# Reordering the start of a two-layer attention and gMLP kernel: x, wq and wk loaded first, one weight scaled at a time, the other weights' loads tied to the loop's steps

## The chip, the cores and the metric

The kernel runs on one core of a Trainium2 chip. The metric is the device time of one execution in microseconds (us). The engines of the core work beside each other and wait for each other through semaphores: TensorE (PE, matrix products; PEld is its loading of weights), VectorE (DVE), ScalarE (ACT), GpSimd (POOL), and SyncE (SP), whose queue issues the DMA transfers of this kernel one after the other.

## The reference

The input x is 2048 × 640 in float32. Four residual steps follow, an attention A and a gated MLP B, each twice with the same weights:

```python
x = x + A(layernorm(x));  x = x + B(layernorm(x))
x = x + A(layernorm(x));  x = x + B(layernorm(x))

def A(x):                      # 32 heads of 20, 4 segments of 512 rows
    q, k, v = x @ wq, x @ wk, x @ wv          # each 640 x 640
    for s in range(4):
        a_dot = softmax(q_s k_s^T * 20**-0.5 + causal mask) @ v_s
        a_mem = phi(q_s) M / (phi(q_s) z + 1e-6)
        o_s   = g * a_mem + (1 - g) * a_dot   # g = sigmoid(beta), by head
        M, z  = M + phi(k_s)^T v_s, z + sum(phi(k_s))
    return o @ wo

def B(x):                      # w_in 640 x 1728, w_sp 2048 x 2048, w_out 864 x 640
    z = gelu(x @ w_in)
    return (z[:, :864] * (w_sp @ layernorm(z[:, 864:]) + b_sp)) @ w_out
```

## The kernel before

All large products are made of 16-bit halves: each float32 operand is scaled and split into a high and a low part (h and l at the end of a tile's name), and three products are summed. A weight is scaled by a power of two that comes from its largest absolute value. For one weight that is: loads of 128 × 640 rows into a staging tile, a maximum of each on DVE, `pow2_scales` (a transpose and a product on PE and seven small instructions on DVE, lines 52 to 65, ending in `iv`), and `split_scaled` for each of five row blocks (high part on ACT, line 72; low part on DVE, line 73).

`prologue` does this for wv, wq and wk at the start (loads line 135, maxima line 138), and makes some scalars from the scales (lines 150 to 165). Each layer is then one attention (`Attention.run`), one stretch for the output projection and w_in, and one for w_sp and w_out. The weights wo, w_in and w_out are split once and the halves are kept in DRAM; the second layer loads these (line 96).

In the attention, x comes in 16 tiles of 128 rows, four to a segment. `prep` loads a tile (line 608), takes its statistics (lines 202 to 205), normalizes it (line 616), splits it (lines 217, 218) and turns it by a DMA transpose (line 219). `value(t)` makes the values of a tile (vps, 30 matmuls, line 633). `unit(s, m)` makes q and k of segment s for 128 of the 640 columns (qps and kps, 15 matmuls each, line 690), which go as qhl and khl (line 707) to a stack in DRAM (`st`, lines 799, 800), and phi of k as phl (line 724). Each of the 64 head pairs (16 per segment) then fetches its rows from the stack (`qk<-st`, line 810), is multiplied for its row maxima (mp, line 828; mx on DVE, line 872), gets its `mr` (DVE, line 893, with the transfer `qk<-mr` to the pair's tile), and makes and uses its probabilities (P, PH, PL, pv). One mr stands for one pair, so these instructions mark progress.

The loop in `run` has three steps t to a pair, from a negative start to about 200. At each step, four generators add work that is due: `fills` (prep of later x tiles, loads of o), `background`, `dense` (values and units of the next segment) and `reads`. `background` is tied to steps only by the number it yields. At its start it runs `other_scales`: 32 loads of wo, w_in and w_out into two staging buffers (tile `wmst`, line 179), each with a maximum (`wap`, lines 181 and 185), and the scale chain at step 53. From step 55 on it loads and splits wo and the second half of w_in (tiles `wst`, lines 106, 72, 73) and stores the halves (line 111); in the second layer it loads them.

The order on PE is the program's own: `manual_schedule(engines=ENGINES)` holds only PE to it. For DVE, ACT, POOL and SP a list scheduler sets the order, by priority and by when it expects an operand. What is due at a later step of `background` can therefore stand far ahead of that step on SP and DVE.

## Time and profile before

| | us |
|---|---|
| three runs before, median (lowest to highest) | 2440.96 (2439.71 to 2448.43) |
| the profiled execution's own time | 2440.32 |
| its span in the trace | 2438.6 |
| PE busy | 2218.2 |
| DVE busy | 1434.3 |
| first value matmul | 36.33 |
| first matmul of unit (0,2) | 88.20 |
| mr of pair 1, first attention | 123.85 |
| mr of pair 1, second attention | 1313.42 |

The page gives busy time by engine, the chain of work that ended last, and the costliest groups of instructions. A group's row reads: line, engine, operation, output<-inputs, shapes, count | busy us, mean ns of one | idle time of the engine ahead of them and what ended it. A row of the table of windows reads: stretch, its length, busy us of PE, PEld, DVE, ACT and POOL with the number of instructions, PE's granted clock, busy share of the DMA engines, GB/s. A row of the timeline reads: start, duration, engine, line, operation; SPq is the issue of a transfer. A row of the chain reads: start, length, what it was.

### The profile page before, as it was taken

To read this page: it belongs to the slowest core of one execution; us is meant where nothing else is said; L and a number is where in the kernel's file an instruction comes from. 1 tells how busy PE (TensorE), PEld (TensorE's weight loads), DVE (VectorE), ACT (ScalarE), POOL (GpSimd) and SP (SyncE) were. 2 spreads that over 40 slices of the span, in tenths; PEclk is the share of its full clock that TensorE was granted. 3 is DMA by queue.
4 is the path that set the end of the run, shared out by engine and by line. 5 is a ranking of instruction groups with operands and counts; after the bars stand their busy time and mean duration, and the time that the engine had idled before them with its cause. 6 is when DMAs were issued, how large, how long until landed. Compare 5 with 4: busy or idle time off the path is not lost.

```text
span 2438.6 us, 50718 instructions
## 1 busy us (share of the span) xinstructions
PE 2218.2 (91%) x20682; PEld 1319.0 (54%) x20682; DVE 1434.3 (59%) x2766; ACT 1133.7 (46%) x1388; POOL 936.1 (38%) x728
## 2 busy tenths in 40 slices
PE   3698789999899989999997989999988997999998
PEld 2355455666555545555554556565654554555554
DVE  8668878777654555444326777877764452454441
ACT  3278777777632222212124988777762221121110
POOL 3168678888610100000002988887871010000000
PEclk9899999999999999999999999999998998999999
DMA  6824634344553488766445253443455345665762
GB/s 196 214 57 109 162 115 122 93 117 133 146 143 107 113 223 206 171 157 164 114 127 133 77 119 88 113 109 93 123 160 124 88 108 165 163 169 155 175 127 58
DMA packets 502505, 325.00 MB, mean 133 GB/s; under 512 B 408512, under 2 KB 443456, under 8 KB 497152
## 3 DMA queue, kind: packets, MB, share of 16 engines
q1 hardware_dynamic: 502272, 321.76, 51.4%
q8 instruction: 162, 2.65, 0.5%
q14 instruction: 71, 0.58, 0.1%
HBM read 148.25 MB, written 85.34 MB: 96 GB/s over the span
## 4 chain that ended last, share of the span: by engine, by line
PE 60%; DVE 11%; DMA 11%; ACT 7%; issue 5%; POOL 3%; SPq 3%; ACTq 0%; DVEq 0%; POOLq 0%
PE gp L380 16%; PE zp L295 14%; PE cyp L409 6%; PE pv L909 3%; PE yps L666 3%; PE kps L690 3%; DMA wr<-in_B_w_sp_dram 3%; PE vps L633 3%; PE mp L856 3%; PE qps L690 3%; ACT PH L882 2%; ACT P L865 2%; PE es L856 2%; POOL PL L883 2%; DVE mx L872 2%
## 5 line engine op out<-in xcount | busy, mean ns | idle before, releaser
L883 POOL TENSOR_TENSOR PL<-P,PH 128x1280 f16<-128x1280 f32 x248 | 649.8, 2621 | 155.2 <-ACT PH L882 145.6
L380 PE MATMUL gp<-zh,wt 128*128 128x432 f16 x2048 | 466.5, 348 | 24.0 <-DMA wt<-wn 24.0
L872 DVE TENSOR_REDUCE mx<-mp 128x2 f32<-128x1024 f32 (+3 forms) x512 | 409.4, 818 | 108.1 <-PE mp L828 106.2
L380 PEld LDWEIGHTS <-wt 128*128 128x128 f16 x3072 | 301.8, 98 | 286.5 <-DMA wt<-wn 25.7
L865 ACT ACTIVATE P<-es,sc 128x1024 f32<-128x1024 f32 (+1 forms) x384 | 370.3, 964 | 128.5 <-PE es L828 122.6
L882 ACT CAST PH<-P 128x1280 f16<-128x1280 f32 x256 | 320.5, 1253 | 19.0 <-PE pv L909 12.0
L295 PEld LDWEIGHTS <-th 128*128 128x128 f16 x1920 | 188.9, 99 | 177.8 <-issue 11.7
L380 PE MATMUL gp<-zl,wt 128*128 128x432 f16 x1024 | 272.8, 348 | 0.0
L395 POOL MEMSET un<- 128x64 f16 x32 | 4.8, 151 | 675.7 <-DMA ut<-un 588.9
L205 POOL TENSOR_TENSOR lnrs<-lnve,mhalf 128x1 f32<-128x1 f32 x96 | 58.6, 618 | 484.6 <-DVE lnve L204 459.6
L856 PEld LDWEIGHTS <-qk 60*128 60x128 f16 (+1 forms) x2048 | 93.0, 94 | 222.2 <-issue 155.1
L357 DVE TENSOR_REDUCE am<-wr 128x1 f32<-128x2048 f32 x32 | 73.2, 2286 | 214.7 <-DMA wr<-in_B_w_sp_dram 214.6
L383 ACT ACTIVATE u<-gp,bsp,un 128x864 f32<-128x864 f32 x32 | 34.2, 1068 | 355.5 <-PE gp L380 355.5
L409 PE MATMUL cyp<-wuh,ut 128*128 128x320 f16 (+1 forms) x896 | 166.8, 303 | 15.4 <-DMA ut<-un 15.4
L633 PE MATMUL vps<-wvh,xt 128*128 128x320 f16 x640 | 156.3, 310 | 22.5 <-DMA xt<-xnhl 13.8
L856 PE MATMUL es<-qk 64*128 64x512 f16 (+3 forms) x1024 | 135.2, 299 | 41.6 <-ACT P L865 26.9
L409 PEld LDWEIGHTS <-ut 128*128 128x128 f16 (+1 forms) x1344 | 132.6, 99 | 73.7 <-DMA ut<-un 17.4
L909 PE MATMUL pv<-vs,PL 128*128 128x41 f16 x2560 | 163.8, 181 | 7.3 <-POOL PL L883 4.5
L909 PE MATMUL pv<-vs,PH 128*128 128x41 f16 x2560 | 167.8, 182 | 1.2 <-DVE ab L925 1.2
L828 PEld LDWEIGHTS <-big 64*128 64x128 f16 x3072 | 141.7, 95 | 49.8 <-issue 3.1
L856 PE MATMUL mp<-qk 60*128 60x512 f16 (+3 forms) x1024 | 137.8, 306 | 31.1 <-DVE mx L872 28.6
L367 ACT ACTIVATE wn<-wr,ivw 128x1024 f16<-128x1024 f32 x64 | 71.9, 1144 | 194.6 <-DVE ivw L362 111.1
(182 smaller groups left out, 4138.5 us busy)
## 6 DMA issues: line engine op xcount, KB each, us to landing
wr<-in_B_w_sp_dram SPq DMA_DIRECT2D x32, 1024.0 KB
qk<-st SPq DMA_DIRECT2D x256, 120.0 KB
x<-x SPq DMA_DIRECT2D x56, 320.0 KB
z<-z SPq DMA_DIRECT2D x32, 432.0 KB
cz<-z SPq DMA_DIRECT2D x32, 432.0 KB
xt<-in_A_x_dram SPq DMA_DIRECT2D x32, 320.0 KB
st<-qhl SPq DMA_DIRECT2D x40, 256.0 KB
st<-khl SPq DMA_DIRECT2D x40, 256.0 KB
```

The costliest lines, as they stand in the source:

```text
L295: nc.tensor.matmul(zp[:, n, :FHH], a[:, k, :], b[:, k, c:c + FHH], start=(k == 0 and j == 0), stop=(k == KD - 1 and j == 2))
L380: nc.tensor.matmul(gp[:, n, :FHH], wt[:, k // 8, a, k % 8, :], b[:, k, n * FHH:(n + 1) * FHH], start=(k == 0 and j == 0), stop=(k == NT - ...
L409: nc.tensor.matmul(yp[:, n, :320], a[:kn[k], k, :], b[:kn[k], k, n * 320:(n + 1) * 320], start=(k == 0 and j == 0), stop=(k == KO - 1 and ...
L633: nc.tensor.matmul(ps, a[:, k, c], b[:, k, n * 320:(n + 1) * 320], start=(i == 0), stop=(i == 14))
L690: nc.tensor.matmul(ps, a[:, k, c], b[:, k, :], start=(i == 0), stop=(i == 14))
L828: nc.tensor.matmul(out, g.big[r, 64 - 64 * s:192 - 64 * s], mk, start=False, stop=s == 1, skip_group_check=True)
L856: nc.tensor.matmul(out[:, h, o:o + w], a[r, ac], b[r, bc], start=o == 0, stop=False, skip_group_check=True)
L865: nc.scalar.activation(P[:, :, 512 * c:512 * c + ew], es[:, :, :ew], AF.Exp, scale=g.esc)
L872: nc.vector.tensor_reduce(self.mx[m][:, :, i], mp[:, :, o:o + w], AX.X, ALU.max)
L882: nc.scalar.copy(PH, P[:, h])
L883: (nc.gpsimd if h == 0 or n < self.N - self.TAIL else nc.vector).tensor_tensor(PL, P[:, h], PH, ALU.subtract)
L909: nc.tensor.matmul(pv[:, i, h, :], x[:, c:c + 128], v[:, j, h0 + h, :], start=(j == 0 and x is PH), stop=(j == i and x is PL), skip_group_ ...
```

## The change

`prologue` becomes `attn_weights`, which only makes tiles, `attn_scalars`, and a method `head` that the first attention runs ahead of its loop, at high priority. `head` loads the first four x tiles, then wq and wk; the wv loads are held behind the last transpose of x. The four tiles get one power instruction together. The weights are then taken one at a time: maxima of q, scale of q, split of q, maxima of k behind the second split of q, and so on, with the four unit products of (0,0) and (0,1) placed between. The values of the four tiles come last.

`other_scales` starts at step −10 with three quarters of a step between loads. Each of its maxima is held behind the last mx or vs instruction of DVE added so far (`self.dve`), and whatever `fills` and `background` add is held behind the last fetch or mr transfer of SP (`self.sp`). That hold applies to both attentions. Memory for wo and the second half of w_in is opened after the head.

```diff
...
-def prologue(g, ctx, wv, wq, wk, wo, w_in, w_out):
+def attn_weights(g, ctx, wv, wq, wk, wo, w_in, w_out):
 
     nc, tc = g.nc, g.tc
-    wp = ctx.enter_context(tc.tile_pool(name="wqkv", bufs=1))
-    g.w = {}
+    wp = ctx.enter_context(tc.tile_pool(name="wqkv", bufs=1, reuse_waits="tile"))
+    g.raw = {"q": wq, "k": wk, "v": wv}
+    g.w = {nm: tuple(wp.tile([128, KD, D], F16, name=f"w{nm}{p}") for p in "hl") for nm in "vqk"}
...
-    nc.vector.memset(g.wap, 0.0)
     g.wam = wp.tile([128, 8], F32, name="wam")
-    with tc.tile_pool(name="wpro", bufs=1, side="right", reuse_waits="tile") as p, \
-            tc.tile_pool(name="wpp", bufs=1, space=PSUM, reuse_waits="tile") as pp:
-        am = p.tile([128, 4, KD], F32, name="wamk")
-        st = {}
-        for i, (nm, dram) in enumerate((("v", wv), ("q", wq), ("k", wk))):
-            st[nm] = p.tile([128, KD, D], F32, name="wst" + nm)
-            for k in range(KD):
-                nc.sync.dma_start(st[nm][:, k, :], dram[k * 128:(k + 1) * 128, :])
-        for i, nm in enumerate("vqk"):
-            for k in range(KD):
-                nc.vector.tensor_reduce(am[:, i, k:k + 1], st[nm][:, k], AX.X, ALU.max, apply_absolute_value=True)
-            nc.vector.tensor_reduce(g.wam[:, i:i + 1], am[:, i], AX.X, ALU.max)
-            pow2_scales(g, p, pp, "wsc", g.wam, i, 1)
-            h = wp.tile([128, KD, D], F16, name=f"w{nm}h")
-            l = wp.tile([128, KD, D], F16, name=f"w{nm}l")
-            for k in range(KD):
-                split_scaled(g, h[:, k], l[:, k], st[nm][:, k], i)
-            g.w[nm] = (h, l)
-
-    pq, pk = g.pw[:, 1:2], g.pw[:, 2:3]
...
+def attn_scalars(g):
+
+    nc = g.nc
+    pq, pk = g.pw[:, 1:2], g.pw[:, 2:3]
...
-def other_scales(g, stage, pool, psum, tag):
+def other_scales(g, a, pool, psum, tag):
 
     nc = g.nc
     last = None
...
         for k in range(w.nk):
             n = min(128, w.dram.shape[0] - 128 * k)
             for c in range(0, w.cols, width):
-                t = stage.tile([128, D], F32, tag="bg", name="wmst")[:n, :width]
+                t = a.bg.tile([128, D], F32, tag="bg", name="wmst")[:n, :width]
                 nc.sync.dma_start(t, w.dram[k * 128:k * 128 + n, w.c0 + c:w.c0 + c + width])
                 if last is not None:
-                    nc.vector.tensor_reduce(*last, AX.X, ALU.max, apply_absolute_value=True)
+                    with g.tc.issue_after(a.dve):
+                        nc.vector.tensor_reduce(*last, AX.X, ALU.max, apply_absolute_value=True)
                 last = g.wap[:n, i, j:j + 1], t
                 yield True
                 j += 1
...
+    def head(self):
+
+        g, nc, tc = self.g, self.nc, self.tc
+        abs_max = lambda out, a: nc.vector.tensor_reduce(out, a, AX.X, ALU.max, apply_absolute_value=True)
+        with ExitStack() as ctx:
+            p = ctx.enter_context(tc.tile_pool(name="wpro", bufs=1, side="right", reuse_waits="tile"))
+            ctx.enter_context(tc.high_priority(offset=HP))
+            xs = self.p3.tile([128, 4, D], F32, tag="P", name="xs")
+            hl = self.p3.tile([128, 4, 2, D], F16, tag="P", name="xhl")
+            for t in range(4):
+                nc.sync.dma_start(xs[:, t], self.x[t])
+            st = {nm: p.tile([128, KD, D], F32, name="wst" + nm) for nm in "qkv"}
+
+            def load(nm):
+                for k in range(KD):
+                    self.sp = nc.sync.dma_start(st[nm][:, k, :], g.raw[nm][k * 128:(k + 1) * 128, :]).ins
+
+            def largest(nm, behind):
+                a = p.tile([128, KD], F32, tag="wamk" + nm, name="wamk")
+                with tc.issue_after(behind):
+                    for k in range(KD):
+                        nc.vector.tensor_reduce(a[:, k:k + 1], st[nm][:, k], AX.X, ALU.max, apply_absolute_value=True)
+                i = WNAMES.index(nm)
+                return nc.vector.tensor_reduce(g.wam[:, i:i + 1], a, AX.X, ALU.max).ins
...
+            load("q")
+            load("k")
+            sx = p.tile([128, 4, 2, 6], F32, name="sx")
+            mv = p.tile([128, 4, 2], F32, name="mvx")
+            rs = p.tile([128, 4], F32, name="rsx")
+            for t in range(4):
+                for i in range(2):
+                    nc.vector.bn_stats(sx[:, t, i, :], xs[:, t, i * 320:(i + 1) * 320])
+                nc.vector.bn_aggr(mv[:, t], sx[:, t])
+            nc.vector.tensor_scalar(rs, mv[:, :, 1], EPS, XS ** -2, ALU.add, ALU.mult)
+            nc.gpsimd.tensor_tensor(rs, rs, g.mhalf.to_broadcast((128, 4)), ALU.pow)
+            for t in range(4):
+                i = nc.vector.tensor_scalar(xs[:, t], xs[:, t], mv[:, t, 0:1], rs[:, t:t + 1], ALU.subtract, ALU.mult)
+                nc.scalar.copy(hl[:, t, 0], xs[:, t])
+            for t in (2, 0, 3, 1):
+                (nc.gpsimd if t > 1 else nc.vector).tensor_tensor(hl[:, t, 1], xs[:, t], hl[:, t, 0], ALU.subtract)
+            for t in (0, 1, 2, 3):
+                o = self.xt[0][:, :, :, t * 128:(t + 1) * 128]
+                last = nc.sync.dma_start(o.rearrange("p i k c -> p (i k) c"), hl[:, t].rearrange("p i c -> p (i c)"), transpose=True).ins
+            with tc.issue_after(last):
+                load("v")
+            qp = self.pe.tile([128, 2, 512], F32, tag="es", name="qp")
+            kp = self.px.tile([128, 2, 512], F32, tag="mp", name="kp")
+            largest("q", i.ins)
+            scale("q")
+            i = split("q")
+            largest("k", i[1])
+            units("q", 0, qp)
+            scale("k")
+            units("q", 1, qp)
+            i = split("k")
+            attn_scalars(g)
+            largest("v", i[-1])
+            units("k", 0, kp)
+            scale("v")
+            units("k", 1, kp)
+            split("v")
+            for t in range(4):
+                for _ in self.value(t):
+                    pass
+                if t == 0:
+                    self.start()
 
     def prep(self, t):
...
                         yield 3 * 136
...
-                nc.vector.scalar_tensor_tensor(v[:, :, DH + 1:], ps, QS, v[:, :, 0:DH], ALU.mult, ALU.subtract)
+                self.dve = nc.vector.scalar_tensor_tensor(v[:, :, DH + 1:], ps, QS, v[:, :, 0:DH], ALU.mult, ALU.subtract).ins
...
-    def unit(self, s, m):
+    def unit(self, s, m, own=None):
 
         g, nc = self.g, self.nc
         xh, xl = self.xt[s % 2][:, 0], self.xt[s % 2][:, 1]
-        for nm in ("q", "k"):
+        for nm in ("q", "k") if own is None else own:
             wh, wl = g.w[nm]
-            ps = self.pd.tile([128, L], F32, tag="dn", name=f"{nm}ps")
+            ps = self.pd.tile([128, L], F32, tag="dn", name=f"{nm}ps") if own is None else own[nm]
...
-            self.nc.sync.dma_start(self.qk[n % self.NQK][64 * h:64 * h + 60], self.st[n // 16 % 2][c:c + 20].rearrange("p l i c -> (p l) i c"))
+            self.sp = self.nc.sync.dma_start(self.qk[n % self.NQK][64 * h:64 * h + 60], self.st[n // 16 % 2][c:c + 20].rearrange("p l i c -> (p l) i c")).ins
 
...
-                nc.vector.tensor_reduce(self.mx[m][:, :, i], mp[:, :, o:o + w], AX.X, ALU.max)
+                self.dve = nc.vector.tensor_reduce(self.mx[m][:, :, i], mp[:, :, o:o + w], AX.X, ALU.max).ins
...
-            nc.sync.dma_start(self.qk[n % self.NQK][60 + i:125 + i:64, 0].rearrange("h (t c) -> h t c", t=4), mr[:, i])
+            self.sp = nc.sync.dma_start(self.qk[n % self.NQK][60 + i:125 + i:64, 0].rearrange("h (t c) -> h t c", t=4), mr[:, i]).ins
...
         def background():
 
-            g = self.g
-            yield 6
+            g, nc = self.g, self.nc
+            yield -10
             if not g.wo.made:
-                for i, _ in enumerate(other_scales(g, self.bg, self.pl1, self.pm, "ms")):
-                    yield 6 + 1.2 * i if _ else 53
+                nc.vector.memset(g.wap, 0.0)
+                for i, _ in enumerate(other_scales(g, self, self.pl1, self.pm, "ms")):
+                    yield -10 + 0.75 * i if _ else 53
+                nc.sync.dma_start(g.bsp, self.b_sp.rearrange("(t p) -> p t", p=128))
             yield 54
             for j, (w, width, pace) in enumerate(((g.wo, D, 1.3), (g.wi[1], FHH, 3))):
                 w.tiles(g.top[j])
...
                     yield 55 + 14 * j + pace * i
 
         if self.stacked < 0:
-            for t in range(0, 4, 2):
-                for f in zip(self.prep(t), self.prep(t + 1)):
-                    f[0]()
-                    f[1]()
-                if t == 0:
-                    self.start()
-            for i in range(4, 8):
-                self.early(i)
+            self.head()
         else:
             self.start()
+        g = self.g
+        g.top = [self.top.enter_context(g.tc.tile_pool(name=n, bufs=1, side="right", reuse_waits="tile")) for n in ("topi", "topo")][::-1]
         streams = [[next(it), i, it] for i, it in enumerate((fills(), background(), dense(), reads()))]
 
         def until(t):
...
                 e = min(streams)
                 if e[0] >= t:
                     return
-                e[0] = next(e[2], None)
+                with self.tc.issue_after(self.sp) if e[1] < 2 and self.sp is not None else ExitStack():
+                    e[0] = next(e[2], None)
                 if e[0] is None:
                     streams.remove(e)
...
```

Three places show the order. The first is PE at the start; wtp and wbc are the two products of a scale chain. Before, the last two chains and the first value product:

```order
L58 MATMUL wbc<-wdg,ones_68 128x1
L52 MATMUL wtp<-ident,wam 1x128
L58 MATMUL wbc<-wdg,ones_68 128x1
L633 LDWEIGHTS xt_302
L633 MATMUL vps<-wvh,xt_302 128x320
```

After, the end of the first product of q (qp), the chain of k and the beginning of the second:

```order
L757 MATMUL qp<-xt_172,wqh 128x512
L757 LDWEIGHTS wql
L757 MATMUL qp<-xt_172,wql 128x512
L52 MATMUL wtp<-ident,wam 1x128
L58 MATMUL wbc<-wdg,ones_68 128x1
L757 LDWEIGHTS wqh
L757 MATMUL qp<-xt_172,wqh 128x512
```

Before, three scale chains are followed by 120 matmuls for values and then by those of units (0,0) and (0,1), 15 for each q and k. After, the chain of q is followed by 15 matmuls for q, the chain of k, 15 for q and 15 for k, the chain of v, the last 15 for k, and then the 120 for values. From unit (0,2) on both are the same.

The second place is the start of SP's queue, with the loads of weights, x and wmst. Before:

```order
L479 DMA gate<-in_A_beta_dram 128x32
L135 DMA wstv<-in_A_wv_dram 128x640 x5
L135 DMA wstq<-in_A_wq_dram 128x640 x5
L135 DMA wstk<-in_A_wk_dram 128x640 x5
L1108 DMA bsp<-in_B_b_sp_dram 128x16x1
L608 DMA xt<-in_A_x_dram 128x640 x2
L179 DMA wmst<-in_A_wo_dram 128x640 x5
```

After:

```order
L601 DMA xs<-in_A_x_dram 128x640 x4
L606 DMA wstq<-in_A_wq_dram 128x640 x5
L606 DMA wstk<-in_A_wk_dram 128x640 x5
L466 DMA gate<-in_A_beta_dram 128x32
L645 DMA_TRANSPOSE xt_172<-xhl 128x10x128 x4
L606 DMA wstv<-in_A_wv_dram 128x640 x5
```

x stands first, wv behind the transposes, and wmst comes later: two loads before the first pair's fetches and nine more before the first mr transfer, where there were 32.

The third place is DVE around the first mr instruction. Before, at the last maxima (line 185 is the last of them, line 187 begins the scale chain):

```order
L181 TENSOR_REDUCE wap<-wmst 128x1
L616 TENSOR_SCALAR xt<-xt,lnmv,lnrs 128x640
L185 TENSOR_REDUCE wap<-wmst 96x1
L187 TENSOR_REDUCE wam<-wap 128x4
L872 TENSOR_REDUCE mx<-mp 128x2 x2
L788 TENSOR_TENSOR mst_299<-mup,bmask 128x147
L707 SCALAR_TENSOR_TENSOR khl<-kps,khl 128x512
L712 TENSOR_SCALAR kps<-kps,sc 128x512
```

After, from the first mr on (line 960 is now mr, 939 mx, 168 the maxima):

```order
L960 SCALAR_TENSOR_TENSOR mr<-mtp,mr 8x128
L706 SCALAR_TENSOR_TENSOR vs<-vps,vs 128x16x20
L939 TENSOR_REDUCE mx<-mp 128x2 x2
L168 TENSOR_REDUCE wap<-wmst 128x1
L774 SCALAR_TENSOR_TENSOR qhl<-qps,qhl 128x512
L939 TENSOR_REDUCE mx<-mp 128x2
L168 TENSOR_REDUCE wap<-wmst 128x1 x2
L855 TENSOR_TENSOR mst_169<-mup,bmask 128x168
L939 TENSOR_REDUCE mx<-mp 128x2
L168 TENSOR_REDUCE wap<-wmst 128x1
L774 SCALAR_TENSOR_TENSOR khl<-kps,khl 128x512
```

Before, all 32 maxima are done ahead of the first mr. After, 21 stand behind it, four to a pair, between mx, qhl and khl. Further on, the splits of wo stand in pairs 20 to 23, and those of the second half of w_in, before within pairs 19 to 25, one per two pairs from 24 to 42. In the second attention the four loads of kept halves (line 96), before ahead of its loop, stand behind step 54, between the fetches and mr transfers of pairs 18 to 20.

34 lines of the change are left out of this document (21 added, 13 removed).

## The prediction

> **What bounds the kernel now.** I read the page's busy shares first, then the chain of waits from 0 to 130 us, then a table of windows over the same stretch, then the groups and the single instructions.
>
> ```profile
> span 2438.6 us, 50718 instructions
> PE 2218.2 (91%) x20682; PEld 1319.0 (54%) x20682; DVE 1434.3 (59%) x2766; ACT 1133.7 (46%) x1388; POOL 936.1 (38%) x728
> ...
> core 0: us, PE busy (x) PEld busy (x) DVE busy (x) ACT busy (x) POOL busy (x), PEclk, DMA share, GB/s
> 0.00:20.00 20.00, 3.47 (x12) 2.57 (x12) 17.29 (x50) 5.45 (x8) 5.34 (x25) 1.00 0.85 279
> 20.00:40.00 20.00, 4.63 (x17) 2.67 (x18) 19.55 (x53) 7.94 (x12) 5.83 (x7) 1.00 0.52 151
> 80.00:100.00 20.00, 14.55 (x69) 6.71 (x69) 9.52 (x18) 4.60 (x8) 1.94 (x2) 0.84 0.94 235
> 100.00:120.00 20.00, 9.48 (x60) 4.75 (x59) 14.01 (x25) 3.58 (x7) 0.55 (x1) 0.74 0.73 209
> 1250.00:1260.00 10.00, 10.00 (x74) 7.02 (x72) 5.24 (x11) 5.74 (x9) 4.36 (x6) 1.00 0.99 318
> ```
>
> PE is 91% busy over the span, so little can be won except where it idles: the head. For the first 40 us PE works 8.1 us and DVE 36.8: DVE sets the pace, and the chain of waits names its instructions. From about 52 us on the chain runs over transfers instead:
>
> ```profile
> 45.92 3.59 PE vps L633 x15
> 52.09 4.04 DMA xt<-xnhl
> 59.82 3.51 DMA xt<-in_A_x_dram
> 73.25 3.81 DMA wmst<-in_B_w_in_dram
> 78.18 3.63 DMA wmst<-in_B_w_in_dram
> 95.47 0.82 DVE wap L181
> 98.78 4.01 DMA wmst<-in_B_w_out_dram
> 105.64 3.55 DMA wmst<-in_B_w_out_dram
> 120.93 1.33 PE vps L633 x9
> ...
> 315.50 2.51 DMA wst<-in_B_w_in_dram
> ```
>
> These are the x tiles, and the weights for the later phases (tile wmst, two buffers), whose maxima stand in DVE's order between instructions of the attention. The landmarks are PE's first matmul of unit (0,2), from which on PE's order is the same before and after, and the mr instruction of each head pair (here pairs 1, 7, 19 and 28 of the first attention and the same four of the second), with the issue of one kept weight between them:
>
> ```profile
> 88.20 0.38 PE L690 MATMUL qps<-xt,wqh 128*128 128x512 f16 x1
> 123.85 0.27 DVE L893 SCALAR_TENSOR_TENSOR mr<-mtp,mr 8x128 f16<-8x128 f32 x1
> 168.15 0.27 DVE L893 SCALAR_TENSOR_TENSOR mr<-mtp,mr 8x128 f16<-8x128 f32 x1
> 254.04 0.27 DVE L893 SCALAR_TENSOR_TENSOR mr<-mtp,mr 8x128 f16<-8x128 f32 x1
> 350.91 0.27 DVE L893 SCALAR_TENSOR_TENSOR mr<-mtp,mr 8x128 f16<-8x128 f32 x1
> 1249.68 0.32 SPq L96 DMA_DIRECT2D wol<-w_ol  x1
> 1313.42 0.27 DVE L893 SCALAR_TENSOR_TENSOR mr<-mtp,mr 8x128 f16<-8x128 f32 x1
> 1359.21 0.27 DVE L893 SCALAR_TENSOR_TENSOR mr<-mtp,mr 8x128 f16<-8x128 f32 x1
> 1444.01 0.27 DVE L893 SCALAR_TENSOR_TENSOR mr<-mtp,mr 8x128 f16<-8x128 f32 x1
> 1519.87 0.27 DVE L893 SCALAR_TENSOR_TENSOR mr<-mtp,mr 8x128 f16<-8x128 f32 x1
> ```
>
> The second attention has no weights to fetch or scale, so it prices those of the first. Pair 1 to 19 takes 130.2 us in the first (254.04 − 123.85) and 130.6 in the second; pair 19 to 28 takes 96.9 and 75.9. Scaling and splitting wo and half of w_in there costs 21 us.
>
> **Term 1, the start up to unit (0,2).** DVE's work in the head, by groups over 0 to 90 us, ACT's split (line 72), the first maximum, and the first and last step of the scale chain of v:
>
> ```profile
> L181 DVE TENSOR_REDUCE wap<-wmst 128x1 f32<-128x432 f32 x20 | 11.5, 587 | 2.4 <-DMA wmst<-in_B_w_in_dram 2.4
> L202 DVE BATCH_NORM_STATS2 lnst<-xt 128x6 f32<-128x320 f32 x18 | 7.9, 479 | 8.1 <-DMA xt<-in_A_x_dram 8.1
> L616 DVE TENSOR_SCALAR xt<-xt,lnmv,lnrs 128x640 f32<-128x640 f32 x9 | 5.5, 609 | 3.6 <-POOL lnrs L205 3.6
> L73 DVE SCALAR_TENSOR_TENSOR wvl<-wstv,iv,wvh 128x640 f16<-128x640 f32 x5 | 4.2, 861 | 0.0
> L138 DVE TENSOR_REDUCE wamk<-wstq 128x1 f32<-128x640 f32 x5 | 4.0, 804 | 0.0
> L72 ACT ACTIVATE wqh<-wstq,iv 128x640 f16<-128x640 f32 x5 | 3.7, 816 | 7.4 <-DVE iv L65 7.4
> ...
> 5.36 0.82 DVE L138 TENSOR_REDUCE wamk<-wstv 128x1 f32<-128x640 f32 x1
> 10.02 0.16 DVE L139 TENSOR_REDUCE wam<-wamk 128x1 f32<-128x5 f32 x1
> 15.18 0.14 DVE L65 TENSOR_SCALAR iv<-iv 128x1 f32<-128x1 f32 x1
> ```
>
> The first loaded tile is used at 5.36 us; x now stands in that place. From there, DVE in its new order: four tiles of statistics, 8 × 0.48 plus aggregates, to about 10 us; POOL's power and four normalizations of 0.6, to 13; two differences and five maxima of wq of 0.8, to 19. The scale chain of v took 5.3 us (10.02 to 15.32), with five maxima of wq between its steps, 4.0 in all; with nothing between it needs at least the remaining 1.3 and at most 5.3, and since it crosses to PE and back twice I take 3. So the scale of q is there at 22. The five splits of q (0.86 each, after ACT's first of 0.82) and the five maxima of k between them give 30.5; the scale of k, 33.5; its splits and the 15 small scalars, 41; the maxima of v and the first unit's results, 46; the scale of v, 49.5; its splits among the results of units (0,0) and (0,1), 57. The 60 unit matmuls run on PE meanwhile and hide. Only the values remain: 120 matmuls, of which 105 come after the last split; at 1.33/9 = 0.148 us that is 15.5. Unit (0,2) starts at about **73** instead of 88.2: **−15** (65 to 80, that is −23 to −8). The x tiles, first in the queue and turned by about 24 us, are no longer waited for; the wv loads, behind the transposes in SP's queue, land near 30 and have until 41. The high and low copies of x on ACT (640 columns each, like its split of 0.82) and POOL are covered by DVE's maxima; uncovered they cost about 3.
>
> **Term 2, unit (0,2) to the first mr.** Today 123.85 − 88.20 = 35.7 us, and PE is 47 to 73% busy in the two windows that cover it. The waits of 60 to 130 us say why:
>
> ```profile
> PE kps L690 <- DVE phl L724: 17.9, 3, 9.5
> DVE wap L181 <- DMA wmst<-in_B_w_out_dram: 7.9, 4, 6.3
> ```
>
> DVE stood 7.9 us before maxima whose transfers had not landed, with khl and phl queued behind it, and PE waited for phl. In the changed order the last 9 maxima ahead of the first mr are of wo and w_in instead of w_out, again between qhl, khl and phl. If they never stall, all 7.9 go; if they stall as now, nothing. A transfer is shorter than the w_out ones, but there are as many: I take **−5** (−9 to 0).
>
> **Term 3, pairs 1 to 7.** Before, all 32 loads and maxima came ahead of the first mr. Now 11 do (two in the head), and 21 stand behind it, four per pair. Each load waits in SP's queue for its buffer, and the mr and qk transfers of the next pairs stand behind it there; each maximum waits in DVE's queue for its load, and mx stands behind that. With two buffers a load has a cycle of its landing (2.5 to 4.0 in the chain rows), its maximum (0.6 to 0.8) and 0.3 of issue, halved: 1.7 to 2.5 us, 2.15 at the middle. 21 loads then last 36 to 53 us, against the 5.25 pairs of 7.4 (44.3/6), 39 us, beside which they run: 0 to +14. I take **+6**, the middle, since the queues are emptier there than at 92 to 110 us (0.94 DMA share at 80 to 100).
>
> By the Trainium skill, page "DMA: Bandwidth & Descriptors", section "Anatomy of one DMA — SWDGE (gpsimd) path", a transfer takes about 2.0 us plus its bytes at 436 GB/s, which would be 2.7 us for these loads and make this term about 0; these go by another path, and the chain's landings of 3.6 to 4.0 lie above it.
>
> **Term 4, pairs 19 to 44.** wo's splits keep their place; those of w_in now stand one per two pairs (24 to 42) instead of crowded in 19 to 25. Of the 21 us above at most 18 could go (the scale chain stays), at least none. The splits themselves are long there:
>
> ```profile
> L73 DVE SCALAR_TENSOR_TENSOR wi1l<-wst,iv,wi1h 128x432 f16<-128x432 f32 x10 | 12.4, 1247 | 4.8 <-ACT wi1h L72 4.8
> ```
>
> 432 columns take 1.25 us, while 640 took 0.86 in the head, where POOL has little to do. I take **−8**, a little under half. The Trainium skill, page "SBUF — State Buffer", section "Who interferes with whom", says that a DVE instruction with two SBUF inputs and a GpSimd instruction that reads SBUF shut each other out. The rows agree, and by it spreading would not shorten a split, since POOL works on until pair 54; the sum would be some 3 us higher.
>
> **Term 5, the second attention.** The kept split weights (four loads, two of 640 × 640 and two of 640 × 864 halves of two bytes, 3.85 MB) were issued around 1250 us, where PE was busy 10.00 of 10: they cost nothing. Their new place is behind step 54 of the second attention, ahead of mr transfers. There 3.85 MB at the 318 GB/s of that window is 12 us of all queues, for which qk<-mr can wait. The nearest row is the first attention's pairs 26 to 28, where two stores of the same tiles fall. I take **+5** (0 to 12). x loads tied to steps: ±3.
>
> The bsp load and the memset of wap move into the loop, one instruction each: nothing. PE's matmuls are the same in number and, from unit (0,2) on, in order.
>
> Sum: −15 − 5 + 6 − 8 + 5 = −17. The profiled execution took 2440.32 us, 1.7 more than its span and 0.6 below the median of 2440.96. So **2423 us**; half the width of the terms (8, 5, 7, 9, 6 and 3), added as independent errors, is ±16.
>
> **The rivals.** (a) The loop's loads hide and the spreading pays in full: DVE has 41% idle time over the span, and the second attention's pairs show what pairs cost without them. Term 3 is 0, term 4 −14: 2411. Against it is that the loop's DVE order is fixed, and a late load stops it. (b) The order of loads and maxima becomes a chain of its own: every load behind step −10 waits for the maximum two loads earlier, and if SP stands with the mr transfer behind it, so that only one load is under way at a time, 21 loads take 21 × (3.3 + 0.8) = 86 us instead of the 44.3 of these pairs. That is +42 in place of term 3: 2423 − 6 + 42 = 2459, slower. The other terms are worth −23, so the sign turns at 1.1 us exposed per load. For it: in-order queues on both sides, and 6.3 us already waited at once. Against: two buffers, and no mr transfer waits behind more than two loads in SP's order. (c) The head's gain isn't kept: the x tiles behind unit (0,2) are loaded no earlier than now (59.82), so that what starts at 73 waits for them, and term 1 shrinks to −4: 2434, no change. Against it is that the first four tiles alone feed everything up to the first mr, and that the queues are free of the other weights until then.
>
> **How the numbers follow.** A difference under 0.5% (12.2 us) counts as none here. Forecast 0.58, (a) 0.18, (b) 0.12, (c) 0.12. With ±16 around 2423, two thirds of the forecast lie under 2428.8 and nearly all the rest is no change. Faster: 0.39 of the forecast, (a), and 0.03 of (c), 0.60; same: 0.18 and the other 0.09, 0.27; slower: (b) and a little, 0.13. The range reaches from under (a) to where (b) has only part of its price: 2400 to 2448.
>
> **What would show it.** Right: PE's first qps of unit (0,2) at 65 to 80 us; the first mr 28 to 35 us behind it; pair 1 to 7 in 44 to 59 us; pair 19 to 28 near 80 with a few us more up to pair 44; pair 18 to 22 of the second attention longer by about 5. Wrong: DVE idle before maxima of wmst for over 20 us after the first mr (b), or idle before 57 us in the head, which would mean that another engine or a transfer sets its pace.

## The result and the profile after

The changed kernel takes 2449.78 us in the median (2443.51 to 2458.71, 20 runs), the kernel before 2442.89 (2439.42 to 2450.36, 20 runs). The ratio is 1.0029, 95% interval 1.0020 to 1.0038: 7 us more, where 18 less were forecast, and just outside the range. It is under the 0.5% that the prediction counted as none. The profiled execution took 2455.51 us with a span of 2453.7, 5.7 over the median, and that of the kernel before lay 2.6 under its own; so some 8 of the 15.1 us between the two spans belong to these executions. A second pair of traces (below) is 10.4 apart.

The same landmarks as before (unit (0,2) on PE; mr of pairs 1, 7, 19, 28 and 44 of the first attention; pairs 1, 19 and 28 of the second), and pair 44 of the kernel before, which stood in no row yet. First the rows of the changed kernel's timeline:

```profile
72.89 0.59 PE L757 MATMUL qps<-xt,wqh 128*128 128x512 f16 x2 [0.77 <-DVE vs L706]
104.95 0.27 DVE L960 SCALAR_TENSOR_TENSOR mr<-mtp,mr 8x128 f16<-8x128 f32 x1
163.13 0.27 DVE L960 SCALAR_TENSOR_TENSOR mr<-mtp,mr 8x128 f16<-8x128 f32 x1
248.06 0.27 DVE L960 SCALAR_TENSOR_TENSOR mr<-mtp,mr 8x128 f16<-8x128 f32 x1
345.39 0.27 DVE L960 SCALAR_TENSOR_TENSOR mr<-mtp,mr 8x128 f16<-8x128 f32 x1
491.63 0.27 DVE L960 SCALAR_TENSOR_TENSOR mr<-mtp,mr 8x128 f16<-8x128 f32 x1
1322.92 0.27 DVE L960 SCALAR_TENSOR_TENSOR mr<-mtp,mr 8x128 f16<-8x128 f32 x1
1454.42 0.27 DVE L960 SCALAR_TENSOR_TENSOR mr<-mtp,mr 8x128 f16<-8x128 f32 x1
1535.78 0.27 DVE L960 SCALAR_TENSOR_TENSOR mr<-mtp,mr 8x128 f16<-8x128 f32 x1
```

And of the kernel before:

```profile
488.12 0.27 DVE L893 SCALAR_TENSOR_TENSOR mr<-mtp,mr 8x128 f16<-8x128 f32 x1
```

| stretch | before, us | after, us | difference |
|---|---|---|---|
| start to unit (0,2) | 88.2 | 72.9 | −15.3 |
| unit (0,2) to mr of pair 1 | 35.7 | 32.1 | −3.6 |
| pair 1 to 7 | 44.3 | 58.2 | +13.9 |
| pair 7 to 19 | 85.9 | 84.9 | −1.0 |
| pair 19 to 28 | 96.9 | 97.3 | +0.4 |
| pair 28 to 44 | 137.2 | 146.2 | +9.0 |
| second attention, pair 19 to 28 | 75.9 | 81.4 | +5.5 |

So the first mr comes 19 us earlier, and the stretches of the two loops give back 28. Of the 6 us that are left of the spans' difference, 5.6 stand between w_sp's first product and the second attention's first mr (449.6 before, 455.2 after). Where 1 to 7 lost its time, the table of windows of the changed kernel shows for that stretch (after the length: PE, PEld, DVE, ACT, POOL busy, then PE's granted clock), and its waits:

```profile
104.90:163.10 58.20, 43.98 (x551) 27.00 (x548) 43.66 (x85) 34.30 (x44) 28.91 (x16) 0.91 0.60 149
...
DVE wap L168 <- DMA wmst<-in_B_w_in_dram: 8.5, 9, 2.2
...
DVE wap L168 <- DMA wmst<-in_B_w_out_dram: 2.1, 3, 0.9
```

The same stretch of the kernel before:

```profile
123.90:168.10 44.20, 40.16 (x552) 25.27 (x550) 30.25 (x58) 32.10 (x42) 25.08 (x13) 1.00 0.29 64
```

DVE is busy 13.4 us longer and stands 10.6 us before maxima whose loads have not landed (and 0.8 before the last one, line 172). Either number would explain most of 13.9 us. PE's granted clock is 0.91 in this stretch, against 1.00 before. Which of the two counts is what the experiments had to tell apart.

### The profile page after: what moved, and what is told of

Read it like the earlier page. It is cut to its first block, busy times and chain, and to the rows that moved or that the text cites. A ratio compares the mean times of both kernels' runs of the same rounds, so it can differ in the third digit from the quotient of the medians.

```text
span 2453.7 us, 50694 instructions
## 1 busy us (share of the span) xinstructions
PE 2233.6 (91%) x20682; PEld 1326.4 (54%) x20682; DVE 1435.9 (59%) x2765; ACT 1134.5 (46%) x1388; POOL 934.2 (38%) x723
## 5 line engine op out<-in xcount | busy, mean ns | idle before, releaser
L976 PE MATMUL pv<-vs,PL 128*128 128x41 f16 x2560 | 164.1, 182 | 6.1 <-POOL PL L950 3.7
```

What stands on the lines that cost most here:

```text
L976: nc.tensor.matmul(pv[:, i, h, :], x[:, c:c + 128], v[:, j, h0 + h, :], start=(j == 0 and x is PH), stop=(j == i and x is PL), skip_group_ ...
```

## The experiments

All times are medians of four or ten runs; each ratio is to runs of the kernel before on the same chip, with its 95% interval.

**Without the loads.** In `other_scales`:

```diff
-                t = a.bg.tile([128, D], F32, tag="bg", name="wmst")[:n, :width]
-                nc.sync.dma_start(t, w.dram[...])
-                if last is not None: ...
-                        nc.vector.tensor_reduce(*last, AX.X, ALU.max, ...)
-                last = g.wap[:n, i, j:j + 1], t
```

> The changed kernel without the 32 loads and 32 maxima of wo, w_in and w_out in the attention's loop (their scales are then a constant, so the later weights are split at another scale; nothing else is left out). Theory A (the 21 loads and maxima behind the first mr hold up DVE and with it the pairs): pairs 1 to 7 take 44 us again instead of 58, and the time is 14 to 18 us under the changed kernel, 2432 to 2436. Theory B (the first pairs are slow because the head's end and the fill of x for the next segment now fall into them): pairs 1 to 7 stay at 54 or more, the time at 2446 or more.

Measured: 2424.20 us, ratio 0.9913 (0.9881 to 0.9945). Pairs 1 to 7 take 44.8 us. Theory A holds, and the time is 8 us under what it expected: the first mr is 5 us earlier than in the changed kernel (100.1), and pairs 19 to 28 take 92.2. Nothing else that fell into the first pairs slows them.

**Fewer to a pair.**

```diff
-                    yield -10 + 0.75 * i if _ else 53
+                    yield -10 + 1.8 * i if _ else 53
```

> The changed kernel with 1.8 steps between two loads instead of 0.75, so that fewer than two fall into a pair, up to pair 16; all are still there. Theory A with the wait as its price (each maximum waits for a load that came too late for its place): with two pairs' time for a load nothing waits, pairs 1 to 19 take about 134 us instead of 143, the time is about 2440. Theory A with the occupancy as its price (a maximum of 0.6 to 0.8 us delays the row maxima wherever it stands): the same 13 us are spread over 16 pairs, the time stays at 2450.

Measured: 2444.13 us, 0.9996 (0.9985 to 1.0006). Pairs 1 to 7 improve to 47.6, but 7 to 19 rise from 84.9 to 99.4: the loss moves with the loads. Against the expectation of the waiting theory the waits did not vanish: 13.3 us are still spent before maxima. In this trace SP issues the loads only 2 to 4 us ahead of the maxima that wait, behind an mr transfer (two at 149.3 us, for a maximum at 151.9 that had waited 2.2), although the maxima now stand further apart. So this run did not separate the two prices.

**The maxima alone.**

```diff
+                if last is None:
+                    one = a.bg.tile([128, D], F32, tag="bg", name="wmst")
+                    nc.sync.dma_start(one, w.dram[0:128, 0:D])
-                t = a.bg.tile([128, D], F32, tag="bg", name="wmst")[:n, :width]
-                nc.sync.dma_start(t, w.dram[...])
+                t = one[:n, :width]
```

> The changed kernel with all 32 maxima of the other weights in their places, but 31 of the 32 loads left out: every maximum reads one tile that is loaded once at the start (so the scales of the later weights are wrong, nothing else is left out). No maximum has a transfer to wait for. Occupancy theory (what counts is the 13.9 us for which the 21 maxima keep DVE busy between row maxima): pairs 1 to 7 take 55 to 59 us as with the loads, the time stays within 5 us of the changed kernel, 2445 to 2452. Waiting theory (what counts is the 10.6 us for which DVE stands before maxima): pairs 1 to 7 take 44 to 49 us and the time is 2436 to 2440. Both count alike: 50 to 54 us.

Measured: 2430.82 us, 0.9943 (0.9924 to 0.9962). Pairs 1 to 7 take 49.2 us: of the 13.4 us between this stretch without any of it (44.8) and the changed kernel (58.2), 4.4 are the maxima themselves and 9.0 their loads. DVE is busy as long as in the changed kernel, 42.5 us against 43.7, so most of its added work is hidden when it needn't wait. The stretch lies at the upper edge of what the waiting theory expected (44 to 49), the time below it. This version is 19 us under the changed kernel, although DVE has the same instructions.

**Deep staging.** Eight buffers in memory that wo and w_in take later, each load six places ahead, the second attention free as in a run below:

```diff
-                t = a.bg.tile([128, D], F32, tag="bg", name="wmst")[:n, :width]
+                t = a.stage.tile([128, D], F32, tag="wm", name="wmst")[:n, :width]
...
-                if last is not None:
+                held.append((g.wap[:n, i, j:j + 1], t))
+                if len(held) > 6:
                     with g.tc.issue_after(a.dve):
-                        nc.vector.tensor_reduce(*last, ...)
+                        nc.vector.tensor_reduce(*held.pop(0), ...)
...
+            self.stage = deep.enter_context(g.tc.tile_pool(name="wmx", bufs=8, side="right", reuse_waits="tile"))
...
-                    yield -10 + 0.75 * i if _ else 53
+                    yield -10 + 0.75 * max(0, i - 6) if _ else 53
+                deep.close()
+                g.top = tops()
```

> The changed kernel with the second attention free and eight staging buffers in place of two for the loads of wo, w_in and w_out (in memory that wo's and w_in's halves take later); each load is issued six places ahead of its maximum, the maxima stay four to a pair, a few places later. If the waits for these loads were two thirds of the loss, as the run with maxima alone says, pairs 1 to 8 take 5 us more than the 51.2 of before, no maximum waits, and the time is 2422 to 2432. If the transfers' traffic cost it and not the waits, it stays near 2442.

Measured: 2433.84 us, 0.9958 (0.9942 to 0.9975); pairs 1 to 7 take 50.1 us with all transfers there. The waits that name mx or the maxima, of 97 to 154 us, are

```profile
PE mp L925 <- DVE mx L941: 7.3, 9, 2.5
...
DVE mx L941 <- PE mp L897: 5.1, 6, 1.5
...
PEld L925 <- DVE mx L941: 4.1, 6, 1.5
```

and no maximum of wmst stands among them, although 21 of them are in the stretch as in the changed kernel. With all transfers there it is 0.9 us longer than with the maxima alone, so the traffic costs next to nothing. Being late for the places of their maxima in DVE's order costs 7 to 9 us: the stretch took 56.9 us with the second attention free and two buffers, 58.2 in the changed kernel. The time stays 2 us above what was expected.

**The head alone.** Nothing held, neither loads nor maxima, and the start (step 6) and pace of before:

```diff
-                with self.tc.issue_after(self.sp) if e[1] < 2 and self.sp is not None else ExitStack():
+                with ExitStack():
...
-                    yield -10 + 0.75 * i if _ else 53
+                    yield 6 + 1.2 * i if _ else 53
```

> The new head alone: nothing is held, and other loads are paced as in the kernel before, so that all 32 stand ahead of the first mr again and the splits of w_in within five pairs. If the head is worth 15 us and the loop's new order costs the rest, unit (0,2) starts at 73 and the time is 2425 to 2432. If the 32 loads and maxima only move out of the head's shadow, the first mr is as late as 118 to 124, and the time is 2438 to 2444.

Measured: 2440.34 us, 0.9988 (0.9975 to 1.0002). The second case: the scheduler puts all 32 loads ahead of the first mr, DVE takes 21 of the maxima before unit (0,2), and that unit starts where it did before the change. From the timeline and from the groups of 0 to 88.4 us:

```profile
88.39 0.38 PE L756 MATMUL qps<-xt,wqh 128*128 128x512 f16 x1
...
L167 DVE TENSOR_REDUCE wap<-wmst 128x1 f32<-128x432 f32 (+1 forms) x21 | 13.5, 645 | 7.7 <-DMA wmst<-in_B_w_in_dram 7.7
```

13.5 us of maxima and 7.7 of waits for them stand where the head had won its time. The first mr is at 122.1.

**The loop alone.** The kernel before, with its own prologue, and this change's `other_scales`, pace and holds (the second attention free):

```diff
-            yield 6
+            yield -10
...
-                    yield 6 + 1.2 * i if _ else 53
+                    yield -10 + 0.75 * i if _ else 53
...
-                e[0] = next(e[2], None)
+                with self.tc.issue_after(self.sp) if e[1] < 2 and self.sp is not None and first else ExitStack():
+                    e[0] = next(e[2], None)
```

> The kernel before, with its old head, and the changed kernel's loop: other weights' loads and maxima tied to steps, fills and background held in the first attention, the second free. Beside the run with the second attention free it prices the new head alone. If the head is worth its 15 us with this loop, unit (0,2) starts at 85 to 90 us, the first mr comes at 118 to 122, and the time is 2455 to 2460. If it was the 32 loads and not the order of the head that made the start long, unit (0,2) starts at 72 to 78 and the time is 2442 to 2446.

Measured: 2451.68 us, 1.0028 (1.0015 to 1.0042). Neither case came whole. Unit (0,2) starts at 75.4 us (the second case), but the first mr is at 116.5 (nearly the first), because the old head's x tiles and phi are late there: PE waits 9.3 us for phl and 5.8 behind a statistics step of x. Beside the run with the second attention free (2442.19) the new head is worth 9 to 10 us. The four corners:

| | unit (0,2), us | mr of pair 1, us |
|---|---|---|
| before | 88.2 | 123.9 |
| new head alone | 88.4 | 122.1 |
| new loop alone | 75.4 | 116.5 |
| both (second attention free) | 71.7 | 104.0 |

**The second attention free.**

```diff
-                with self.tc.issue_after(self.sp) if e[1] < 2 and self.sp is not None else ExitStack():
+                with self.tc.issue_after(self.sp) if e[1] < 2 and self.sp is not None and first else ExitStack():
...
+        first = not g.wo.made
```

> The changed kernel, with fills and background held behind SP's last fetch in the first attention alone; in the second the scheduler places them as before. Theory C (the kept weights' loads in the middle of the second attention and x held to its steps cost time there): the 6 us lost in pairs 19 to 24 and the 5 lost ahead of the second attention's first mr come back, the time is 2439 to 2442. Theory D (these 11 us are a lower granted clock in that execution and not the order): the time stays at 2448 or more.

Measured: 2442.19 us, 0.9988 (0.9974 to 1.0003), 8 us under the changed kernel. Pairs 19 to 28 of the second attention:

```profile
1449.05 0.27 DVE L960 SCALAR_TENSOR_TENSOR mr<-mtp,mr 8x128 f16<-8x128 f32 x1
1524.72 0.27 DVE L960 SCALAR_TENSOR_TENSOR mr<-mtp,mr 8x128 f16<-8x128 f32 x1
```

75.7 us, as before the change (75.9). Theory C holds for this stretch. The edit frees the kept weights' loads and the x loads together, so it does not say which of them had cost the time. The stretch ahead of the second attention's first mr came down to 452.9, which lies within what other runs show (448.6 to 455.2), so nothing follows for that part.

**The splits.** Several runs were for pairs 19 to 44. In the first, w_in's splits follow each other three times as fast, beside a free second attention:

```diff
-            for j, (w, width, pace) in enumerate(((g.wo, D, 1.3), (g.wi[1], FHH, 3))):
+            for j, (w, width, pace) in enumerate(((g.wo, D, 1.3), (g.wi[1], FHH, 1))):
```

> As the run with the second attention free, but w_in's ten splits follow each other at one step instead of three per half (pairs 24 to 31 instead of 24 to 42). If a split costs the same wherever it stands, pairs 19 to 44 take 242 us as in that run and the time is 2442. If the kernel before was right to crowd them (several splits hide behind one stall), 232 to 236 us and 2433 to 2437. If crowding is what costs, as my prediction said, over 246 us and 2447 or more.

Measured: 2450.28 us, 1.0025 (1.0014 to 1.0035); pairs 19 to 44 take 249.9 us against 242.6. Crowding held splits costs 7 us, as the prediction had it.

In the second, a block is split one place after the next is loaded:

```diff
                 yield
-                split_scaled(self.g, self.h[:n, k, c:c + w], self.l[:n, k, c:c + w], st, self.c)
+                if held:
+                    split_scaled(*held.pop())
+                held.append((self.g, self.h[:n, k, c:c + w], self.l[:n, k, c:c + w], st, self.c))
                 yield
+        split_scaled(*held.pop())
```

> The changed kernel with each block of wo and w_in split one block later than loaded, so that ACT does not stand before the split for its transfer (15 us of such waits between pairs 19 and 44 in the changed kernel's trace). If these waits are the price of the splits' new places, pairs 19 to 44 take 9 to 13 us less than 243.5, and the time is 2437 to 2441. If only the work itself counts, the waits go and the time stays at 2450.

Measured: 2448.81 us, 1.0021 (1.0010 to 1.0031); 239.8 us. It is 3.7 us shorter in that stretch, and the time is not clearly another. But the waits that the edit was to remove are still there. From the waits of 240 to 480 us:

```profile
ACT wi1h L72 <- DMA wst<-in_B_w_in_dram: 9.8, 9, 1.9
...
ACT woh L72 <- DMA wst<-in_A_wo_dram: 7.6, 4, 3.1
```

That is 17.4 us, where the changed kernel has 15.3 between pairs 19 and 44. With deep staging as well:

> The deep staging run with wo's and w_in's splits one block behind their loads as well; fills and splits stay held. If ACT's and DVE's waits for these transfers are what the splits' held places cost, pairs 19 to 44 take 233 to 235 us instead of 237.6 and the time is 2426 to 2430. If the work itself is the cost, it stays at 2432 to 2436.

Measured: 2436.03 us, 0.9964 (0.9950 to 0.9978); 240.2 us, where deep staging alone took 237.6. Here too ACT waits 17.8 us for these loads, with deep staging alone 17.9. Neither run took the waits away, so neither says whether they are the price; that stays untested.

In another, the loads of x and o are free and background alone is held (`e[1] == 1` in place of `e[1] < 2`, with `first`):

> As the run with the second attention free, and fills (loads of x, of o) free too; only background is held. If x tiles that land late hold up DVE (7.5 us of waits in pairs 19 to 44 of the changed kernel, 5.5 before), pairs 19 to 44 take 236 to 239 us instead of 242.6 and the time is 2436 to 2439. If not, 2442.

Measured: 2444.73 us, 1.0006 (0.9993 to 1.0018). Pairs 19 to 44 take 238.1 us, as expected, but the first mr moves from 104.0 to 112.0, with unit (0,2) at 81.4. The gain in one place is lost in the other; that x tiles put into the head delay it was only argued.

Then both kernels once more, unaltered:

> The changed kernel once more, unaltered, for a second trace. If the 9.4 us that pairs 19 to 44 lost are the order's, the stretch takes 242 to 245 us again; if they are this one execution's, 234 to 239. Likewise the stretch from w_sp's first product to the second attention's first mr: 455 again, or 450.

> The kernel before once more, for a second trace: pairs 19 to 44 take 232 to 236 us if that stretch repeats, 1 to 7 take 44, and the time stands at 1.00.

Measured: 2452.06 us, 1.0028 (1.0018 to 1.0039), and 2446.56 us, 1.0003 (0.9989 to 1.0018). Pairs 19 to 44 take 242.8 us (after) and 234.2 (before); pairs 1 to 7 take 58.5 and 44.3. These stretches repeat within 1 us, so the loss is the order's. The stretch ahead of the second attention's first mr is 452.2 and 448.8. Pairs 19 to 28 of the second attention repeat less well: 81.1 (after) and 77.8 (before, 75.9 in its first trace).

**The work at the end.** wo's five maxima early, the other 27 from step 125, a second scale chain, then w_in's splits, at two steps apart where it was three; the second attention free:

```diff
-                for i, _ in enumerate(other_scales(g, self, self.pl1, self.pm, "ms")):
+                for i, _ in enumerate(other_scales(g, self, self.pl1, self.pm, "ms", 0, 1)):
...
+                    for i, _ in enumerate(other_scales(g, self, self.pl1, self.pm, "ms", 1, 4)):
+                        yield 125 + i if _ else 155
...
-                    yield 55 + 14 * j + pace * i
+                    yield (55, 156)[j] + pace * i
```

> A version built from the theory that any of this work costs its own duration in pairs 1 to 44 and nothing in the last segment, where PE is the bound and DVE 40 to 50% busy: the new head; wo's five loads and maxima ahead of the first mr; the 27 of w_in and w_out from step 125 on, then a second scale chain, then w_in's splits up to the end; the second attention free. By the theory the first mr stays at 101 to 105 us, pairs 1 to 19 take 130 us, pairs 19 to 44 some 12 less than 243.5, the last segment is unchanged, and the time is 2440 minus 15 to 30: 2410 to 2425. By its rival (the work finds no free time there either, 27 × 0.65 and 10 × 1.25 us go on top) 2432 to 2440.

Measured: 2459.02 us, 1.0062 (1.0044 to 1.0080). The first half came as expected: pairs 1 to 19 take 131.9 us, 19 to 44 take 229.4, 13 less than in the run it builds on. But the last segment, pairs 44 to 64, takes 196.5 us instead of 160.2. Its window, and that of the kernel before under it:

```profile
463.10:659.60 196.50, 166.98 (x2150) 105.10 (x2149) 148.08 (x280) 125.09 (x152) 132.09 (x89) 0.92 0.57 153
```

```profile
488.10:648.30 160.20, 154.92 (x2157) 100.59 (x2155) 118.18 (x237) 120.47 (x145) 131.25 (x90) 0.99 0.49 133
```

DVE is busy 30 us longer, and the stretch is 36 us longer. The time lies above what the theory (2410 to 2425) and its rival (2432 to 2440) expected. My theory of the last segment fell. What took its place is not settled, because DVE also stands 19.6 us before these maxima in that window, with two buffers and each load one place ahead, as in the changed kernel:

```profile
DVE wap L168 <- DMA wmst<-in_B_w_in_dram: 14.5, 14, 1.9
...
DVE wap L168 <- DMA wmst<-in_B_w_out_dram: 5.1, 4, 2.1
```

So this run doesn't tell work that finds no free time from loads that come late once more. The same places with deep staging were not tried.

**Everything together.** Deep staging, the second attention free, and nothing held but the loads of `other_scales`:

```diff
-                with self.tc.issue_after(self.sp) if e[1] < 2 and self.sp is not None else ExitStack():
+                with self.tc.issue_after(self.sp) if e[1] == 1 and self.sp is not None and first and not g.wo.made and not split_on[0] else ExitStack():
...
+            split_on[0] = True
             yield 54
```

> The version that the runs so far point to: the new head, the deep staging of the run before, and after these loads nothing held, so that the splits and the x tiles go where the scheduler had them in the kernel before. Pairs 1 to 19 as in the deep run (135 us), pairs 19 to 44 as in the kernel before (234) instead of 242: the time is 2414 to 2426. If the scheduler's places for x and o are worse with a fast head, 2430 or more.

Measured: 2427.32 us, 0.9939 (0.9923 to 0.9955), 17 us under the kernel before and faster than both. The first mr is at 106.2 us and pairs 1 to 7 take 46.3, 2.0 more than before the change, with the same 21 maxima in them. Pairs 19 to 44 take 238.6, not 234, so it ends 1 us above the range that was expected. With the maxima spread to two a pair:

> The deep staging with splits and x free, and 1.7 steps between two loads, so that about two maxima fall into a pair, up to pair 12, none of which waits. If the 5 us that maxima cost without waits come from four of them crowding a pair, pairs 1 to 19 take 131 to 132 us instead of 132.4 and the time is 2423 to 2427; if each costs its 0.2 us anywhere, 132.4 and 2427.

Measured: 2435.33 us, 0.9961 (0.9947 to 0.9976). Pairs 1 to 19 take 132.6 us against 132.4: it makes no difference where such maxima stand. The time came out higher, with losses in pairs 44 to 64 (164.1 against 160.9) and behind that no run explains.

## Why the prediction was wrong, point by point

- **Term 1** (−15 to unit (0,2) at 73) came as summed: −15.3, at 72.9. Its steps hold one by one in the changed kernel's timeline: the scale of q is there at 21.2 us (22 was forecast), that of k at 33.9 (33.5), that of v at 49.4 (49.5), the last split of v ends at 56.7 (57):

```profile
21.05 0.15 DVE L65 TENSOR_SCALAR iv<-iv 128x1 f32<-128x1 f32 x1
33.75 0.14 DVE L65 TENSOR_SCALAR iv<-iv 128x1 f32<-128x1 f32 x1
49.23 0.15 DVE L65 TENSOR_SCALAR iv<-iv 128x1 f32<-128x1 f32 x1
55.04 1.66 DVE L73 SCALAR_TENSOR_TENSOR wvl<-wstv,iv,wvh 128x640 f16<-128x640 f32 x2
```

  Its cause needs a correction: by the corners 12.8 of 16.5 us up to unit (0,2) come with the loop's order, which takes maxima out of this stretch, and the new order of the head pays behind it, up to the first mr.
- **Term 2** (−5) was −3.6, but not by its mechanism. DVE stands 7.7 us before maxima in that stretch, nearly as long as before (8.3), now mostly for wo:

```profile
DVE wap L168 <- DMA wmst<-in_A_wo_dram: 7.0, 2, 5.3
```

  By the prediction's own condition (nothing goes if they stall as now) the term was 0, so that it came near is luck. What shortened the stretch stays open.
- **Term 3** (+6, at most 14) was +13.9, and this is one of the two steps that failed: its size. Here the prediction missed by 8 us. The cycle of 1.7 to 2.5 us per load took the buffers as the only limit. Measured are 58.2/21 = 2.8 us, because a load is also issued late, behind what SP's queue holds ahead of it, and then stops DVE at its place. SP's waits in this stretch name the mr transfers (line 962) first:

```profile
SPq L962 <- ACT mr L959: 5.1, 4, 2.0
SPq L962 <- DVE vs L706: 4.4, 3, 2.9
SPq L962 <- DVE mr L960: 3.7, 2, 3.2
```

  Rival (b) described this; its exposed price is 13.9/21 = 0.66 us per load, below the 1.1 from which it would have decided alone. Deep staging and maxima alone split the price: about two thirds waiting, one third work; in the run with everything together, where the x loads are free too, 2.0 us are left. The sum by the Trainium skill's fit ("DMA: Bandwidth & Descriptors", "Anatomy of one DMA — SWDGE (gpsimd) path"), about 0 for this term, did not come out either; no run here tests the fit itself, which is for another path.
- **Term 4** (−8) was +9.4, the other step that failed, in sign and by 17 us. The prediction read 21 us as the price of scaling and splitting in pairs 19 to 28 and let up to 18 of them go by spreading. The run with w_in's splits at the end bounds that: without them, and with a scale chain for wo alone, 19 to 28 takes 90.5 us and 28 to 44 takes 138.9. So in the kernel before the ten crowded splits cost at most 6.4 us (96.9 − 90.5), and there was no more to free. Behind pair 28 eight spread splits cost 7 us (146.2 − 138.9). All traces agree on this: 28 to 44 takes 142.5 to 148.2 us in the twelve that have held splits there, and 136.6 to 138.9 in the six that have none.

  In pairs 19 to 28 spreading freed nothing in the changed kernel (+0.4), though it can: six other runs with the held splits in the same pairs take 92.2 to 94.5 there. The windows of the changed kernel and of the run with fewer loads to a pair:

```profile
248.06:345.39 97.33, 79.98 (x992) 51.93 (x993) 74.49 (x137) 64.78 (x84) 65.75 (x48) 0.84 0.43 115
```

```profile
247.77:340.28 92.51, 77.45 (x992) 50.86 (x993) 68.30 (x137) 63.89 (x84) 66.58 (x48) 0.89 0.45 121
```

  DVE has as many instructions in both, but they take 6.2 us less in the second: wo's five splits 880 ns each against 1225, w_in's first two 668 against 1430, four normalizations of x 1139 against 1556. In the changed kernel one split of w_in runs beside POOL's PL and takes 2.19 us; the next takes 0.67 us:

```profile
321.65 2.62 POOL L950 TENSOR_TENSOR PL<-P,PH 128x1280 f16<-128x1280 f32 x1
322.53 2.19 DVE L73 SCALAR_TENSOR_TENSOR wi1l<-wst,iv,wi1h 128x432 f16<-128x432 f32 x1 [0.65 <-ACT wi1h L72]
```

  The Trainium skill's rule ("SBUF — State Buffer", "Who interferes with whom"), by which such a split and a POOL instruction that reads SBUF shut each other out, agrees with these two rows. That such meetings lengthen the stretch is argued; no run changed them alone. That w_in's splits get little shorter by spreading was right: the group in the changed kernel, over pairs 19 to 44, has 993 ns against 1247 before:

```profile
L73 DVE SCALAR_TENSOR_TENSOR wi1l<-wst,iv,wi1h 128x432 f16<-128x432 f32 x10 | 9.9, 993 | 7.9 <-ACT wi1h L72 7.8
```

  The 2.5 us that this saves stand against 7.8 of waits for ACT's half, 3.0 more than before.
- **Term 5** (+5) was +5.5, or 3.3 by the second pair of traces, and the free second attention took it back. Its mechanism does not show: pairs were to wait for mr transfers, but PE's waits for qk<-mr in pairs 19 to 28 of the second attention are 0.2 us, and 0.8 before. The size was in part luck.
- With terms 3 and 4 as measured the sum would have been −15 − 4 + 14 + 9 + 5 = +9, against 6.9 between the medians.

Why a split behind pair 28 costs what it does stays open. The runs that were to take away the waits for its load did not do so, and free fills change pairs 19 to 44 by 4.5 us; that DVE's exact place between two row maxima decides was only argued. Nor are the scheduler's places better as such: with deep staging, pairs 19 to 44 take 237.6 us with held splits and 238.6 where the scheduler puts them.

## What to carry to other kernels

A transfer that feeds an engine with a fixed order should be issued several places ahead of its use: of the price of 21 loads and maxima with two buffers, more than half went away with eight buffers and no change in work. The price of work put into another engine's idle time should be read with its transfers in time: the same 21 maxima cost 13.9 us in this loop, about 5 when none waited, and 2 in the fastest version. Moving a load's work to another place brings its waits along, as the run with the work at the end shows. And a shorter start must be looked at with what the scheduler will move into it: alone, this one gained nothing at its own end.

## What the runs showed that I had not expected

The stretches of the first attention's loop repeat to within 1 us from trace to trace (pairs 1 to 7: 58.2 and 58.5; 19 to 44: 243.6 and 242.8), so a single trace tells orders apart there that medians of ten runs, 5 to 13 us apart between lowest and highest, do not. And PE's granted clock is lower in some stretches where it waits: 1.00 in pairs 1 to 7 before, 0.91 after, 0.92 in the last segment that was overfilled. It does not go in step with the waits: with deep staging it is 0.97 with PE busy for 41.4 of 50.1 us, with the maxima alone 0.93 with 42.3 of 49.2. What this adds to a stall was not measured.
